# A chunk's output product on TensorE: products of 320 columns in place of pairs of 160

## The chip, the cores and the metric

The kernel runs on one core of a Trainium2 chip. The metric is the device time of one execution in microseconds (us).

## The reference

Two blocks follow each other: a recurrent attention (RWKV-7) and a feed-forward block with the SoLU activation.

```python
# r, k, v, w, a, b: (4, 8, 768, 40) = batch, head, token, channel
for t in range(S):
    y[:, :, t] = einsum('bhd,bhde->bhe', r[t], state)
    Sa = einsum('bhde,bhe->bhd', state, a[t])
    state = state * w[t] - Sa (x) b[t] + v[t] (x) k[t]      # (x): outer product
x = y as (3072, 320)                                        # rows batch*token, columns head*channel
h = x @ w_in                                                # (3072, 1024)
sm = softmax(h)
solu = h * sm
ln = (solu - mean(solu)) / sqrt(var(solu) + 1e-6) * g_ln
out = ln @ w_out                                            # (3072, 320)
```

The change lies in the last product, `ln @ w_out`, of 1024 by 320 for every row.

## The kernel before

**Tiling.** The 768 tokens are cut into chunks of 64 and the four batches into two pairs, so there are 24 steps of work (called `i`), each of which handles 64 tokens of two batches: 128 rows of the output. Inside a chunk the recurrence is solved in closed form with small matrices per head, most of them 64 by 64; TensorE makes them as many small products on quarters of its array (64 rows by 64 columns). The inverse of a triangular matrix that this needs is made on VectorE (`invert`, lines 495 to 526, the groups `prod` and `uu`), a few rows at a time.

**Stages of a chunk.** `norm`, `scores`, `couple`, `close`, `driven`, `solved`, `read` (tiles `py`, `ps`, `px`, `pu`, `pyo`) make the attention. Its result goes through DRAM to be turned (`leave`, `left`). Two steps later `hidden` makes `h`, `highest`, `exped`, `weighed` and `spreadof` make the maximum, the exponentials and the moments, `folded` turns the activations into `lnT` (tiles `plnT`, then `lnT`: eight blocks of 128 by 128), and `output` (lines 845 to 865) makes the output product into the tile `po`. The normalisation's scale is applied when `po` is copied out on ScalarE (line 859, tile `osb`), and two DMAs on the sync queue store the result. g and the mean are folded into the second weight `w2` beforehand: `mean_more` (lines 246 to 255) makes the mean of `w2` with products of 128 by 128 by 320 columns, by the constant matrix `mean`, at about 101 and 121 us.

**The output product.** For each of the eight blocks `f` of 128 hidden columns, `lnT[:, f, :]` (128 by 128) is the stationary matrix and `w2[:, f, :]` (128 by 320) the moving one; the eight accumulate in one PSUM bank. `in_parts` (line 289) cuts such a product into two halves of 160 columns, with the same stationary matrix given twice. The helper `mm` (line 284) issues one product; every product that goes through it carries line 285 in the profile, so that the tiles tell them apart. All data is fp32, and one fp32 product stands in the profile as two weight loads and two matmuls.

**Order of the work.** The order of every engine is written out by hand (`manual_schedule`); nothing is reordered by a planner. In step `i` the chunk whose output is made is `c - 1 = i - 3`. From step 5 to step 22 the eight blocks are cut as six at the end of the step (`FIRST = 6`) and the remaining two in the next step, behind the transposes `pa` and `pkv` (list `rest`); before that and from step 23 on the eight are made at once, in step 25 seven and one. The last chunk is made by `output_last` (line 828), which has halves of its own, in two PSUM tiles, and does not use `in_parts`. `in_parts` is also used in `decay` (line 360, tile `pcum`), for the first steps.

Of the kernel before, what the change touches and what calls it, by code (L numbers as in the profile page):

```python
# [53 lines left out]
def kernel(  # L54
# [25 lines left out]
    NF = DFF // P  # L80
# [60 lines left out]
    w2 = const.tile([P, NF, DM], FP32, name="w2")  # L141
# [126 lines left out]
    def half(p):  # L268
        return slice(C * p, C * p + C)
# [14 lines left out]
    def mm(o, lhsT, rhs, start=True, stop=True):  # L284
        nc.tensor.matmul(o, lhsT=lhsT, rhs=rhs, start=start, stop=stop, skip_group_check=True)  # L285
# [3 lines left out]
    def in_parts(o, lhsT, rhs, start, stop, n=2):  # L289
        width = rhs.shape[-1] // n  # L290
        for x in range(n):
            part = slice(width * x, width * x + width)
            mm(o[:, part], lhsT, rhs[:, part], start and not x, stop)
# [11 lines left out]
    def where_(i):  # L305
        return i % NPAIR, i // NPAIR
# [7 lines left out]
    def ok(i):  # L314
        return 0 <= i < N
# [529 lines left out]
    def output(i, t, first=NF):  # L845
        if not ok(i):
            return
        d = st[i]
        bp, ci = where_(i)
        t = t[:, 0:DM]  # L850

        def products(lo, hi):
            for f in range(lo, hi):
                in_parts(t, d["lnT"][:, f, :], w2[:, f, :], f == 0, f == NF - 1)
        products(0, first)

        def stored():
            osb = two.tile([P, DM], FP32, tag="osb", name="osb", bufs=1)
            nc.scalar.mul(out=osb, in_=t, mul=d["rs"])
            for p in range(2):  # L860
                nc.sync.dma_start(out=out.rearrange("(b s) n -> b s n", b=B)[2 * bp + p, ci * C:ci * C + C], in_=osb[half(p)])
        if first < NF:
            rest.append((lambda: products(first, NF), stored))
        else:
            stored()
# [303 lines left out]
```

## Time and profile before

| what | value |
|---|---|
| time, median of 3 runs | 535.26 us (533.9 to 539.12) |
| span of the profiled execution | 536.5 us |
| instructions | 28053, of them 12029 matmuls and 12029 weight loads |
| TensorE matmul busy | 480.7 us, 90% of the span |
| VectorE, ScalarE, GpSimd busy | 430.6, 314.1, 227.0 us |
| granted TensorE clock, mean | 0.984 |
| matmuls of `po` at line 285 | 768 records of 160 columns, 115.2 us busy |

The profiled execution's span is 1.2 us above the median of the runs and inside their spread. Busy time of an engine is the union of its records; matmuls are pipelined and their ends are modelled, so that records of one run overlap and the pace must be read from the starts. In the lists, `x768` is the number of records, "128\*128 128x160 f32" is the part of the array used and what is streamed or loaded, and a name behind "<-" in the column of idle time is what ended the wait. PE is TensorE's matmuls, PEld its weight loads, DVE VectorE, ACT ScalarE, POOL GpSimd.

### The profile page before, as it was taken

Reading aid. Unit: us, or ns where it says so; the run is one execution under the profiler, and the core shown is the slowest. Engines: PE = TensorE matmul, PEld = TensorE weight load, DVE = VectorE, ACT = ScalarE, POOL = GpSimd, SP = SyncE. Lnnn points to the kernel's source line nnn. Section 1 sums busy time; section 2 is a strip of 40 time slices with the busy share of each in tenths; the row PEclk is TensorE's granted clock in tenths of the full one; section 3 lists DMA queues with packets and bytes.
Section 4 is the critical chain, followed back from the end, with each engine's and each line's share of the span. In section 5 each row is a group of like instructions: output and inputs, shape, how many; then the busy total and the mean of one; then the engine's idle time right before and its main releaser. Section 6 shows DMA issues by size and latency. Waiting matters only on the chain.

```text
span 536.5 us, 28053 instructions
## 1 busy us (share of the span) xinstructions
PE 480.7 (90%) x12029; PEld 391.0 (73%) x12029; DVE 430.6 (80%) x1752; ACT 314.1 (59%) x627; POOL 227.0 (42%) x376
## 2 busy tenths in 40 slices
PE   4633775798989999999999999999999999999997
PEld 3522665665878878877887887788778877887766
DVE  4599987999997987997998979979989888544322
ACT  3633466488457566556666665666656555654433
POOL 4577538245253344545445263544445331210300
PEclk9999978799999999999999999999999999999999
DMA  8898889765465566674774776675554551421210
GB/s 149 153 157 160 177 142 206 165 134 124 90 131 120 102 125 138 123 151 96 147 156 104 132 150 121 118 155 109 114 118 102 108 111 43 106 65 29 61 53 24
DMA packets 194475, 63.95 MB, mean 119 GB/s; under 512 B 166840, under 2 KB 186528, under 8 KB 194352
## 3 DMA queue, kind: packets, MB, share of 16 engines
q1 hardware_dynamic: 181232, 41.60, 41.8%
q0 software_dynamic: 10768, 19.95, 15.2%
q8 instruction: 94, 1.54, 1.2%
q10 hardware_dynamic: 2352, 0.62, 0.7%
q14 instruction: 29, 0.24, 0.2%
HBM read 47.96 MB, written 14.16 MB: 116 GB/s over the span
## 4 chain that ended last, share of the span: by engine, by line
PE 73%; DVE 17%; DMA 5%; issue 2%; ACT 2%; SPq 0%; POOL 0%; ACTq 0%; POOLq 0%; DVEq 0%
PE po L285 20%; PE h L285 18%; PE px L285 6%; PE pyo L285 5%; PE py L285 5%; DVE prod L516 4%; PE ps L285 4%; DVE uu L519 3%; PE pu L285 3%; PE plnT L804 2%; PE pb L400 2%; PE pa L400 2%; PE psr L285 2%; PE pkv L400 2%; DMA uu_dram<-uu 1%
## 5 line engine op out<-in xcount | busy, mean ns | idle before, releaser
L285 PE MATMUL h<-w_in,xT 64*64 64x512 f32 (+1 forms) x1064 | 121.7, 551 | 0.7 <-issue 0.7
L285 PE MATMUL po<-w,lnT 128*128 128x160 f32 x768 | 115.2, 304 | 0.0
L516 DVE TENSOR_TENSOR prod<-blk,uu 128x48 f32<-128x48 f32 (+19 forms) x576 | 108.1, 227 | 1.3
L285 PEld LDWEIGHTS po<-w,lnT 128*128 128x128 f32 x768 | 105.5, 190 | 4.7 <-issue 0.8
L519 DVE TENSOR_TENSOR uu<-uu,prod 128x48 f32<-128x48 f32 (+19 forms) x576 | 103.8, 219 | 0.0
L483 POOL DMA_DIRECT2D nt_dram<-nt x86 | 50.8, 597 | 84.5 <-ACT nt L475 76.4
L792 POOL TENSOR_TENSOR rs<-var,mhalf 128x1 f32<-128x1 f32 x24 | 17.6, 734 | 138.2 <-ACT var L791 138.1
L761 DVE TENSOR_REDUCE nmax<-h 128x1 f32<-128x1024 f32 x24 | 29.3, 1219 | 32.9 <-PE h L285 32.9
L285 PEld LDWEIGHTS h<-w_in,xT 64*64 64x64 f32 x1064 | 36.7, 133 | 20.4 <-issue 16.7
L790 ACT ACTIVATE sq<-e,mu 128x1024 f32<-128x1024 f32 x24 | 26.9, 1119 | 24.4 <-DVE e L777 24.4
L444 DVE TENSOR_TENSOR lu<-pu,cst 128x512 f32<-128x512 f32 x24 | 16.5, 686 | 26.6 <-PE pu L285 24.8
L769 ACT ACTIVATE e<-h,nmax 128x1024 f32<-128x1024 f32 x24 | 26.7, 1111 | 17.7 <-DVE nmax L761 17.7
L558 ACT ACTIVATE wy<-py,cst 128x256 f32<-128x256 f32 x24 | 11.4, 474 | 39.2 <-PE py L285 37.1
L311 POOL DMA_DIRECT2D raw_r<-in_r_dram x48 | 33.3, 698 | 0.0
L777 DVE SCALAR_TENSOR_TENSOR e<-h,e 128x1024 f32<-128x1024 f32 x24 | 29.2, 1217 | 4.3 <-ACT e L769 4.1
L508 DVE SCALAR_TENSOR_TENSOR uu<-blk,uu 128x30 f32<-128x30 f32 (+3 forms) x144 | 30.2, 262 | 1.7 <-DMA blk<-nt_dram 0.8
L393 POOL TENSOR_TENSOR kb<-raw_b,inv 128x320 f32<-128x320 f32 x24 | 21.4, 894 | 21.1 <-DMA raw_b<-in_b_dram 13.7
L285 PE MATMUL pcum<-lw,cst 128*128 128x160 f32 x48 | 15.1, 461 | 16.7 <-ACT lw L351 16.7
L285 PEld LDWEIGHTS py<-tu,nt 64*64 64x64 f32 x768 | 17.3, 142 | 16.3 <-issue 10.7
L617 ACT COPY st<-psr 128x416 f32<-128x416 f32 (+1 forms) x44 | 14.2, 374 | 24.5 <-PE psr L285 24.4
L664 ACT ACTIVATE x<-px 128x832 f32<-128x832 f32 x24 | 20.7, 864 | 11.0 <-PE px L285 11.0
L710 DVE TENSOR_TENSOR tot<-pyo,st 104x416 f32<-104x416 f32 x44 | 23.8, 581 | 2.9 <-PE pyo L285 2.9
(154 smaller groups left out, 1095.3 us busy)
## 6 DMA issues: line engine op xcount, KB each, us to landing
xT<-x_dram SPq DMA_DIRECT2D x48, 160.0 KB, 4.2
blk<-nt_dram POOLq DMA_DIRECT2D x22, 256.0 KB, 4.7
raw_w<-in_w_dram SPq DMA_DIRECT2D x48, 80.0 KB, 3.3
raw_r<-in_r_dram POOLq DMA_DIRECT2D x48, 80.0 KB, 4.0
lv<-in_v_dram SPq DMA_DIRECT2D x48, 80.0 KB, 3.7
out_dram<-osb SPq DMA_DIRECT2D x46, 80.0 KB, 2.5
a<-in_a_dram SPq DMA_DIRECT2D x44, 80.0 KB, 4.0
raw_k<-in_k_dram SPq DMA_DIRECT2D x42, 80.0 KB, 3.8
```

Of the source, the lines that this page charges most:

```text
L285: nc.tensor.matmul(o, lhsT=lhsT, rhs=rhs, start=start, stop=stop, skip_group_check=True)
L311: queue.dma_start(out=x[half(p), :, 0:D], in_=ap[2 * bp + p, :, ci * C:(ci + 1) * C, :].rearrange("h t d -> t h d"))
L400: nc.tensor.transpose(out=t[0:W2, p, at + C * j:at + C * j + C], in_=x[half(p), 2 * j:2 * j + 2].rearrange("p a b -> p (a b)")[:, skip:ski ...
L483: queue.dma_start(out=blocks[n][e].rearrange("(a x h) s c -> a x s h c", a=GRP, x=2)[at, x], in_=nt[home:home + Q].rearrange("p h j c -> p ...
L508: nc.vector.scalar_tensor_tensor(out=u[:, c, j + 1:Q], in0=nb[:, j, j + 1:Q], scalar=u[:, c, j:j + 1], in1=u[:, c, j + 1:Q], op0=ALU.mult, ...
L516: nc.vector.tensor_tensor(out=ts[-1], in0=nb[:, j:j + 1, j + 1:Q].to_broadcast([P, hi - lo, m]), in1=u[:, lo:hi, j:j + 1].to_broadcast([P, ...
L519: nc.vector.tensor_tensor(out=u[:, lo:hi, j + 1:Q], in0=u[:, lo:hi, j + 1:Q], in1=x, op=ALU.add)
L710: nc.vector.tensor_tensor(out=by_b(tot)[:, :, :, part], in0=y[:, :, :, part], in1=by_b(state_of(i)[:, x])[:, :, :, 0:HW], op=ALU.add)
L761: nc.vector.tensor_reduce(out=nmax, in_=d["h"], axis=AX.X, op=ALU.max, negate=True)
L769: nc.scalar.activation(out=e, in_=d["h"], func=AF.Exp, bias=d["nmax"], accum_out=d["esum"])
L777: nc.vector.scalar_tensor_tensor(out=d["e"], in0=d["h"], scalar=1.0 / DFF, in1=d["e"], op0=ALU.mult, op1=ALU.mult, accum_out=d["mu"])
L790: nc.scalar.activation(out=pair("A" if i == N - 2 else "h", "sq").rearrange("p a b -> p (a b)"), in_=d["e"], func=AF.Square, scale=-float( ...
```

## The change

`output` calls `mm` in place of `in_parts`: each of a chunk's eight blocks is one product of 320 columns instead of two of 160. `output_last`, `decay` and the order of the work are as they were.

```diff
         def products(lo, hi):
             for f in range(lo, hi):
-                in_parts(t, d["lnT"][:, f, :], w2[:, f, :], f == 0, f == NF - 1)
+                mm(t, d["lnT"][:, f, :], w2[:, f, :], f == 0, f == NF - 1)
         products(0, first)
```

## The prediction

> **What bounds the kernel now.** I read the page's busy shares and chain first, then TensorE's waits from 180 us on, then the chain of one pair of steps, and last the records of the output product and of the nearest product with 320 columns.
>
> ```profile
> PE 480.7 (90%) x12029; PEld 391.0 (73%) x12029; DVE 430.6 (80%) x1752; ACT 314.1 (59%) x627; POOL 227.0 (42%) x376
> ...
> PE 73%; DVE 17%; DMA 5%; issue 2%; ACT 2%; SPq 0%; POOL 0%; ACTq 0%; POOLq 0%; DVEq 0%
> ...
> L285 PE MATMUL po<-w,lnT 128*128 128x160 f32 x768 | 115.2, 304 | 0.0
> ```
>
> TensorE is on 73% of the chain that ended last, and the output product (po) is the largest single item of its time: 768 records, 115.2 us. Each fp32 product stands in the trace as two loads and two matmuls, so 768 records are 384 products: 23 chunks of 16, and the last chunk's 16, which another function makes and the change leaves alone. The change touches 23 x 32 = 736 records.
>
> Waits of TensorE from 180 us to the end:
>
> ```profile
> PE py L285 <- issue: 0.9, 2, 0.7
> PE ps L285 <- ACT ex L419: 0.3, 1, 0.3
> ```
>
> In 356 us the matmul stream waited 1.2 us in all. Twenty-one of the 23 chunks are made in that stretch, so whatever their products lose or gain there passes to the end nearly one to one. Only the two chunks at 142 and 163 us lie where other engines still hold TensorE up.
>
> The timeline of TensorE around one chunk, and around the only other full-size products of 320 columns (the mean of the second weight, lines 249 and 253):
>
> ```profile
> 312.63 3.53 PE L285 MATMUL po<-w,lnT 128*128 128x160 f32 x24
> 316.09 0.43 PE L400 MATMUL pa<-cst,a 64*104 64x64 f32 x8
> ...
> 317.12 1.35 PE L285 MATMUL po<-w,lnT 128*128 128x160 f32 x8
> ```
> ```profile
> 142.23 4.51 PE L285 MATMUL po<-w,lnT 128*128 128x160 f32 x32
> ```
> ```profile
> 121.23 0.70 PE L253 MATMUL po<-mean,cst 128*128 128x320 f32 x2
> 121.77 1.78 PE L249 MATMUL po<-w,cst 128*128 128x320 f32 x6
> ```
>
> And the durations of single records, from the view of the tile po (minimum, median, maximum in ns):
>
> ```profile
> L285 PEld LDWEIGHTS po<-w,lnT x768: 186/190/190, 142.1 to 532.2; 128*128 128x128 f32 x192
> L285 PE MATMUL po<-w,lnT x768: 299/299/403, 142.2 to 532.3; 128*128 128x160 f32 x192
> ...
> L249 PE MATMUL po<-w,cst x12: 432/432/537, 101.2 to 123.1; 128*128 128x320 f32 x12
> ```
>
> A record of 160 columns lasts 299 ns and one of 320 lasts 432: 160 more columns cost 133 ns, so streaming 160 columns takes 133 ns and the other 166 ns are the pipeline's length, which overlaps from record to record. The pace is what counts. In the unbroken run of 32 it is (4510 - 299) / 31 = 135.8 ns. For 320 columns, from the start of the first at 121.23 to the modelled end at 123.55, it is (2320 - 432) / 7 = 269.7 ns, with a rounding of some 1.5 ns.
>
> **The change part by part.**
>
> *Removed:* 368 matmul records and 368 weight loads (each chunk's 32 pairs become 16), with the same columns streamed. Two records of 160 take 2 x 135.8 = 271.6 ns; one of 320 takes 269.7. That is 2 ns saved a pair. By the other route, a record of 160 takes 135.8 - 133 = 2.7 ns beyond its stream, and one such excess goes away with each pair. Bounds: 0 if the long record carries twice the excess, and 2.7 ns as all that there is beyond the stream. I take 2.5, nearer to the second route, because the first rests on rounded starts: 368 x 2.5 = 0.9 us, with ends of 0 and 1.0 us.
>
> *The weight loads themselves.* A load's row is 190 ns, longer than the pace of 136, so successive loads overlap each other and the matmuls. What a load costs when nothing covers it is read where a chunk begins: 3530 ns for 24 records is 299 + 23 x 135.8 + 108, so the first load of a run lies open for about 105 ns. The maxima agree: 403 against 299, and 537 against 432, are both 104 or 105 more. That opening load stays, once in each run, before and after. The other loads lie beneath the 133 ns stream of the record ahead, at either width. If that cover were gone for the 320-column record alone, the 368 that remain would cost 368 x 104 = 38 us; the run of six at 121.77 speaks against it, though its stationary matrix is the same constant for all six. Against that stand po's own runs, where a new block of lnT is loaded at every fourth record with no break in the pace.
>
> The Trainium skill ("TensorE: Matmul & The Clock Gate", Back-to-back issue gap) would price this otherwise: a stream of load and matmul pairs at 128 columns is given as about 81 ns a pair against 55.6 for the matmul alone, so the load would cost some 25 ns. By that rule the sum would be an estimated 368 x 25 = 9 us of gain instead of 0.9; the pace of 135.8 against a stream of 133 disagrees with it, but its direction is the second rival below.
>
> *The end of a run.* The last record's modelled end lies 432 ns behind its start instead of 299, but that start is one record of 133 ns earlier. Nobody waits longer. The scaling of the output on ScalarE (osb, line 859) waited 3.3 us for po in eight of its 23 times, off the path; it follows the end of the product as before.
>
> *Order, queues, buffers.* No step moves, no DMA is added, the bank and the 320 columns of the accumulator are the same, and the start mark is still set on the first product only. No wait is added. The sequencer of TensorE gets through a chunk with 64 fewer instructions and is further ahead when it leaves it; that can only let the next loads be ready earlier. I cost it at nothing, because po runs at the stream's pace and the waits above show it ready; what it could give at most is the third rival.
>
> *Sum.* The saving of a run of 24 or 8 is the same 2.5 ns per pair. The profiled execution has a span of 536.5 us, 1.2 us above the median of the runs (535.26) and inside their spread (533.9 to 539.12). 536.5 - 0.9 = 535.6 for a like execution; from the median, 535.3 - 0.9 = 534.4 us. That is 0.2%, and the three runs of the unchanged kernel differ by 1% from lowest to highest, so about 1% is what a measurement of this kernel can tell from no change.
>
> **The rivals.**
>
> *First, slower: the clock.* The granted clock fell to half twice:
>
> ```profile
> 66.90:73.70 6.80, 4.42 (x203) 3.90 (x200) 4.65 (x20) 5.90 (x12) 0.00 (x0) 1.00 0.88 162
> 73.70:80.50 6.80, 5.91 (x113) 5.12 (x112) 6.70 (x31) 3.53 (x7) 4.10 (x8) 0.50 0.74 125
> 80.50:90.80 10.30, 5.48 (x216) 4.68 (x216) 10.09 (x25) 9.30 (x21) 8.86 (x14) 1.00 1.01 228
> 90.80:101.00 10.20, 8.81 (x195) 8.16 (x196) 7.45 (x41) 2.91 (x6) 2.54 (x5) 0.50 0.67 131
> 101.00:536.00 435.00, 422.60 (x10779) 341.73 (x10777) 348.77 (x1407) 263.04 (x525) 171.51 (x270) 1.00 0.53 110
> ```
>
> The columns are the window, its length, busy time and records of PE, PEld, DVE, ACT and POOL, then clock, DMA share and GB/s. Each half-clock window follows one with TensorE busy for 65% or 53%. If the grant goes by issued instructions or loads rather than by time spent streaming, then po, at one record every 270 ns, becomes the sparsest stretch of a steady step. It would show first in the tail, where po and h alternate in runs of 4.5 us. A window of 6.8 or 10.2 us at half clock loses 3.4 to 5.1 us; it decides from two windows on, with 8.5 us: 534.4 + 8.5 = 542.9, and three would give 547. For it: nothing in the trace says what the grant counts. Against it: the columns streamed are the same, the eight records of 320 columns at 121 us ran at clock 1.00, and from 101 us on the clock never fell. The same page of the Trainium skill (Part 1, the HAM clock gate) says that the gate follows how busy TensorE was recently, which agrees with the two drops and leaves this rival little.
>
> *Second, clearly faster: loads hold up the array.* If a removed load costs more than its row shows, the gain is 368 times that. One per cent (5.4 us) needs 14.5 ns, 14% of the 104 ns of an open load; a quarter of it, 26 ns, would give 9.6 us and 525.7 us. Against it stands the 2.7 ns beyond the stream, which leaves nothing to take.
>
> *Third, a little faster: issue.* The chain has 3.8% "issue" between 142 and 225 us, 3.2 us, and 0.65 us after that. If all of it were the sequencer being late and 736 fewer instructions ended it, the gain would be 0.9 + 3.8 = 4.7 us: 530.6 us, still inside 1%. The page's queue 8 fetched 94 packets for 1.54 MB; 736 instructions are 3% of TensorE's 24058, so a proportional share is 0.1 us.
>
> *Fourth: cover lost.* The loads of the long records lie open: 535.3 + 38 = 573 us.
>
> **How the numbers follow.** The forecast gets 0.64, the clock 0.18, the second rival 0.07, the third 0.08, the lost cover 0.03. The forecast and most of the third are within 1%; a fifth of the clock's cases have one window only and also fall there; by the runs' spread a tenth of the forecast's own falls outside, half on each side. That makes slower 0.8 x 0.18 + 0.03 + 0.03, some 0.21, rounded up to 0.22, faster 0.07 + 0.03 + a little of the third = 0.11, within 1% 0.67. The unknown price of a pair alone spans 534.3 to 535.3; the runs' spread of 1% around the forecast gives 530 to 540. Up to 543, where the clock's two windows lie, the range holds some 8 in 10.
>
> **What would show it.** In the changed profile: po with 400 records, 368 of 320 columns at 432 ns and the last chunk's 32 of 160 at 299; a run of 12 lasting 3.50 us where 24 lasted 3.53, and 4 lasting 1.34 or 1.35; po's loads down from 768 to 400, now standing apart, so with a busy time near 368 x 190 ns + 4 = 74 us instead of 105.5; PE's waits after 180 us still near 1 us; the clock at 1.00 from 101 us on. Wrong would be: a pace of 320-column records well off 270 ns (second or fourth rival), a window of clock 0.50 after 142 us (first), or TensorE waiting more than 2 us for another engine after 180 us, which no step here provides for.

## Result and profile after: slower by two thirds of a per cent

| kernel | median | lowest to highest | runs |
|---|---|---|---|
| before | 536.36 us | 533.9 to 539.12 | 6 |
| after | 539.92 us | 537.83 to 541.16 | 6 |

The ratio is 1.0065, with a 95% interval of 1.0038 to 1.0092: 3.5 us slower, inside the range of the prediction but on the other side of 1 than the 0.9 us forecast. A second comparison of the same two kernels (after_again, below) gave 1.0093 (1.0066 to 1.012).

What the prediction said of the product itself came out. From the page of after (busy time, the chain, the groups of po):

```profile
PE 481.0 (90%) x11661; PEld 360.5 (67%) x11661; DVE 431.2 (80%) x1752; ACT 314.4 (59%) x627; POOL 225.1 (42%) x376
...
PE 74%; DVE 17%; DMA 3%; ACT 2%; issue 2%; POOL 0%; ACTq 0%; SPq 0%; POOLq 0%; DVEq 0%
...
L285 PE MATMUL po<-w,lnT 128*128 128x320 f32 (+1 forms) x400 | 114.6, 433 | 0.1
...
L285 PEld LDWEIGHTS po<-w,lnT 128*128 128x128 f32 x400 | 71.1, 190 | 27.9 <-issue 1.2
```

There are 368 fewer records of each kind. The loads now stand apart (27.9 us idle before them, 71.1 us busy). The timeline of TensorE around one chunk:

```profile
313.26 3.50 PE L285 MATMUL po<-w,lnT 128*128 128x320 f32 x12
316.69 0.43 PE L400 MATMUL pa<-cst,a 64*104 64x64 f32 x8
...
317.72 1.34 PE L285 MATMUL po<-w,lnT 128*128 128x320 f32 x4
```

3.50 us where 24 records took 3.53, and 1.34 where eight took 1.35. Steps without any pause last 18.42 us after and 18.46 before. So the product gained its 0.04 us a chunk, and the time was lost elsewhere. TensorE's waits from 142 us to the end, first before, then after, show what kind of time; the columns are what waited, what ended the wait, us in total, times, longest:

```profile
PE py L285 <- issue: 2.1, 3, 1.2
PE pst L400 <- DVE bT L440: 0.5, 1, 0.5
PE pst L400 <- DVE aT L427: 0.3, 1, 0.3
PE ps L285 <- ACT ex L419: 0.3, 1, 0.3
```
```profile
PE pyo L285 <- issue: 1.3, 2, 0.8
PE px L285 <- issue: 0.8, 1, 0.8
PE pst L400 <- DVE bT L440: 0.5, 1, 0.5
PE plnT L804 <- ACT sq L790: 0.4, 1, 0.4
PE pst L400 <- DVE aT L427: 0.3, 1, 0.3
PE ps L285 <- ACT ex L419: 0.3, 1, 0.3
PE h L285 <- issue: 0.3, 1, 0.3
PE py L285 <- issue: 0.2, 1, 0.2
```

No wait for another engine has grown much. What stands there is "issue": TensorE stands still and nothing that the profile shows holds it. In this view it grew only from 2.1 to 2.6 us, because it counts a gap from the modelled end of the matmul ahead and leaves out the short ones; read from the starts of the matmuls, the pauses grew more (the table below). They sit in the middle of rows of equal records, first before, then after:

```profile
347.56 0.48 PE L285 MATMUL py<-uh,wy 64*64 64x32 f32 x18
348.69 0.37 PE L285 MATMUL py<-uh,wy 64*64 64x32 f32 x12 [0.65 <-issue]
```
```profile
194.95 0.71 PE L285 MATMUL pyo<-lv,kb 64*64 64x104 f32 x23
196.49 0.48 PE L285 MATMUL pyo<-lv,kb 64*64 64x104 f32 x9 [0.83 <-issue]
```

A row of 32 records of one kind breaks after the 18th or the 23rd, and the profile shows no wait there.

**What the pauses have in common.** Count TensorE's instructions in the trace from the first one on (loads, matmuls, and its sequencer's semaphore instructions): the two pauses above come after number 15552 and number 7105, which are 256 x 60 + 192 and 256 x 27 + 193. The pages of the profile show an instruction queue, q8, with equal packets (queue, packets, MB, share of the engines' time), before and after:

```profile
q8 instruction: 94, 1.54, 1.2%
```
```profile
q8 instruction: 91, 1.49, 1.1%
```

1.54 MB in 94 packets is 16384 bytes a packet. TensorE's stream has 24235 instructions before and 23516 after; 94 x 256 = 24064 and 91 x 256 = 23296, each less than one block short of it. So q8 carries TensorE's instructions, a packet is a block of 256, and the pauses lie at the ends of blocks. From the packets' times in the trace: a packet starts mostly 0.3 to 2.6 us after TensorE passes a boundary, lasts 0.9 to 1.7 us, and TensorE goes on 1.2 to 1.6 us after a packet's end in 87 of the 88 pauses that the twelve traces show between 171 and 482 us (1.9 us in the other). Added up, some 3.8 us pass in the median from a boundary until the next block can be used, a tenth of the times under 3.1 and a tenth over 4.6. A block of 256 instructions that is over sooner than its successor can be used ends in a pause. Of the 790 blocks that end in the 17 steps counted in the table below, 37 of the 73 that lasted under 3.5 us ended in one, 33 of 249 between 3.5 and 4, 18 of 256 between 4 and 5, and none of the 212 longer ones.

Whether it does depends on what lies in the block. Twelve records of 320 columns with their loads are 24 instructions for 3.5 us; 256 successive instructions of small products can be over in 2.7 us. A steady step of before has exactly 1024 instructions, four blocks. They last 5.97, 4.64, 4.12 and 3.73 us, at the same places in every step, and all are longer than 3.6. The change takes 32 instructions out of a step and brings one wait: 993. Now the boundaries move by 31 a step through the work, some blocks last only 3.0 to 3.6 us, and others over 8.

This is theory F. A reckoning with it: the block times of the trace, a delay taken as 3.6 us with a spread of 0.5 us, and the expected excess summed over all blocks from 175 to 495 us. It gives 3.4 us of pauses for before and 8.7 for after: 5.3 more, from which the 0.9 us of the products goes off. Theory P, the rival: the long products hurt in some other way, or the stretches of half clock before 101 us differ. In the two profiles they do, though up to there the programs are the same. The mean clock from 67 to 101 us is 0.75 before and 0.70 after, and 1.00 later (the columns are those of the prediction's windows; first before, then after):

```profile
67.00:101.00 34.00, 24.52 (x725) 21.76 (x722) 28.78 (x113) 21.54 (x44) 15.51 (x25) 0.75 0.83 165
```
```profile
67.00:101.00 34.00, 25.11 (x726) 23.16 (x721) 30.31 (x118) 22.55 (x45) 16.77 (x25) 0.70 0.82 167
101.00:142.00 41.00, 35.50 (x951) 25.29 (x950) 40.55 (x157) 28.39 (x59) 18.64 (x29) 1.00 0.64 137
142.00:225.00 83.00, 79.75 (x2017) 61.05 (x2016) 71.63 (x298) 52.19 (x107) 35.81 (x58) 1.00 0.57 117
225.00:490.00 265.00, 263.85 (x6952) 195.66 (x6954) 221.33 (x931) 161.72 (x321) 108.58 (x173) 1.00 0.54 114
```

Over all runs the clock was no lower in the slower kernels: on average 0.981 in after_again and 0.980 in before on the same chip, 0.983 in before_dec (below) and 0.982 in before beside it. Only before_nosplit lies lower, at 0.978, and its two runs of the lowest clock (0.965 and 0.968) are not its slowest. So the stretches of half clock do not explain the loss.

### The profile page after: what moved, and what is told of

Same layout as the page of the kernel before. It is cut to its first block, busy times and chain, and to the rows that moved or that the text cites. A ratio compares the mean times of both kernels' runs of the same rounds, so it can differ in the third digit from the quotient of the medians.

```text
span 537.4 us, 27334 instructions
## 1 busy us (share of the span) xinstructions
PE 481.0 (90%) x11661; PEld 360.5 (67%) x11661; DVE 431.2 (80%) x1752; ACT 314.4 (59%) x627; POOL 225.1 (42%) x376
## 4 chain that ended last, share of the span: by engine, by line
PE 74%; DVE 17%; DMA 3%; ACT 2%; issue 2%; POOL 0%; ACTq 0%; SPq 0%; POOLq 0%; DVEq 0%
PE po L285 20%; PE h L285 18%; PE px L285 6%; PE pyo L285 6%; PE py L285 6%; PE ps L285 4%; DVE prod L516 4%; DVE uu L519 3%; PE pu L285 3%; PE plnT L804 2%; PE pb L400 2%; PE psr L285 2%; PE pa L400 2%; DVE uu L508 2%; PE pkv L400 2%
## 5 line engine op out<-in xcount | busy, mean ns | idle before, releaser
L285 PE MATMUL h<-w_in,xT 64*64 64x512 f32 (+1 forms) x1064 | 123.4, 552 | 1.3 <-issue 1.3
L285 PE MATMUL po<-w,lnT 128*128 128x320 f32 (+1 forms) x400 | 114.6, 433 | 0.1
L285 PEld LDWEIGHTS po<-w,lnT 128*128 128x128 f32 x400 | 71.1, 190 | 27.9 <-issue 1.2
L792 POOL TENSOR_TENSOR rs<-var,mhalf 128x1 f32<-128x1 f32 x24 | 15.2, 634 | 136.0 <-ACT var L791 136.0
L285 PEld LDWEIGHTS h<-w_in,xT 64*64 64x64 f32 x1064 | 38.8, 134 | 20.7 <-issue 17.4
L285 PE MATMUL ps<-aT,kvT 40*64 40x64 f32 x768 | 17.5, 230 | 11.4 <-ACT kvT L583 11.1
```

## The experiments

In the table, "late part" is read from each trace, from the turning of the first chunk's activations (the first plnT, near 126 us) to the end; "pauses" counts the block boundaries at which the next matmul starts over 130 ns later than the one ahead of it needs for its stream (0.83 ns a column, from the 133 ns for 160), with the sum of these excesses, in the 17 steps of that part that follow the second. Late part and pauses come from one profiled execution each, while the ratio is over all runs.

```
kernel            instructions   ratio to before (95%)       late part   pauses: number, us
                  in a step
before            1024           1                           410.4       2, 1.3
after             993            1.0065 (1.0038 to 1.0092)   411.8       8, 3.4
after_again       993            1.0093 (1.0066 to 1.012)    414.3       10, 4.7
after_lock        1024           1.0031 (1.0009 to 1.0054)   411.6       6, 3.7
after_waits       1025           1.0005 (0.9983 to 1.0026)   409.7       6, 2.1
after_waits_1024  1024           1.0006 (0.9987 to 1.0026)   410.8       8, 3.4
before_s112       1024, moved    1.0327 (1.0302 to 1.0351)   417.2       8, 5.5
before_s256       1024           1.0621 (1.0594 to 1.0649)   411.2       6, 1.9
before_drift      1056           1.0266 (1.0235 to 1.0298)   426.1       18, 11.9
before_dec        1024, moved    1.007  (1.0046 to 1.0093)   411.0       7, 2.1
before_dec_mean   1024           1.001  (0.9993 to 1.0026)   409.8       3, 0.5
before_nosplit    1016           1.0098 (1.0072 to 1.0123)   416.0       6, 4.3
```

### Instructions added by hand (after_lock, before_s112, before_s256, before_drift)

```diff
+    spare = ctx.enter_context(nc.semaphore())
+    def idle(n):
+        for _ in range(n):
+            nc.tensor.sem_inc(spare)
...
# after_lock, in output: after
                 mm(t, d["lnT"][:, f, :], w2[:, f, :], f == 0, f == NF - 1)
+                idle(3 if lo and f == lo else 4)
# before_s112 and before_s256, ahead of the first loads: before
+    idle(112)      # or 256
# before_drift, in output: before
                 in_parts(t, d["lnT"][:, f, :], w2[:, f, :], f == 0, f == NF - 1)
+                idle(4)
```

> The kernel after (320 columns), with the instructions that the change removed from TensorE's stream put back as increments of a semaphore that nobody waits for: four behind each product of 320 columns, three behind the first of each second part, so that each step again has as many TensorE instructions as in the kernel before, 1024, which is four blocks of 256. Theory F (instruction blocks: a step of 1024 keeps the block boundaries at the same favourable places in every step, the step of 992 lets them wander into the densest stretches, where the next block of instructions comes late): the pauses without a wait go back to those of the kernel before and the 0.9 us of the longer products shows: ratio to before 0.998 (0.996 to 1.000). Theory P (the long products themselves cost elsewhere, or the windows of half clock do): it stays at the ratio of the kernel after, 1.0065 (1.004 to 1.009).

> The kernel before with 112 increments of a semaphore that nobody waits for, once, at the very start of TensorE's stream, while it waits for the first loads. The work is that of the kernel before. Theory F: all block boundaries move by 112 instructions to places where, by the trace of before, the four blocks of a step last 3.6, 3.8, 3.0 and 8.0 us instead of 4.1, 3.7, 6.0 and 4.6; with some 3.6 us from one boundary to the next block's arrival that costs 0.7 us a step, so 13 us in 18 steps: ratio 1.024 (1.012 to 1.032). Theory P: nothing changes, ratio 1.000 (0.998 to 1.002).

> The kernel before with 256 such increments at the start, one whole block: all boundaries fall where they fell. Theory F: ratio 1.000 (0.998 to 1.003), the price of the added instructions alone. If the added instructions as such were what slows the kernel with 112 of them, this one would be slowed more than twice as much. Theory P: 1.000.

> The kernel before (pairs of 160) with four such increments behind each pair, so 32 more instructions a step (1056), all beneath the stream of the output product. The products stay as they were; only the boundaries wander by 32 a step, as in the kernel after, the other way. Theory F: the mean over the places costs 0.2 to 0.4 us a step more than the place of before, 4.4 us in all (2.5 to 7): ratio 1.008 (1.004 to 1.013). Theory P: ratio 1.000.

The tool was too coarse. In the traces the increments follow each other at 150 ns, so 112 of them hold TensorE's first product up to 18.0 us and 256 to 40.3 us, where before begins at 6.7. That is most of what both kernels lost: the first plnT comes at 136.0 and 158.7 us instead of 126.2. In the ratios the prediction for before_s256 was missed altogether. The part behind that mark answers the question: 417.2 us with 112 instructions, 411.2 with 256, 410.4 with none (one trace each). The whole block costs 0.8 us, the part of a block 6.8, with eight pauses of up to 1.4 us, all at one place of the step (the instruction numbers are 448 beyond a multiple of 1024), as in this line of the timeline of before_s112:

```profile
364.71 0.40 PE L285 MATMUL pyo<-lu,kb 64*64 64x104 f32 x6 [1.28 <-issue]
```

The 6.8 us are half of the 13 us that I expected. In before_drift the increments take longer (24 x 150 ns = 3.6 us) than the products they were to hide under (3.3 us), so its 15 us are not a clean test; it has the most pauses of all, 18. after_lock went the way of theory F, to half of the loss (the intervals of after_lock and after overlap), but not to 0.998, and its pauses did not go back to those of before: two pauses of 1.0 and 1.9 us near 400 and 415 us make up most of its 3.7 us. Four increments take 600 ns where the product beside them takes 538, so the sequencer loses its lead, and with it the early request for the next block; that reading is argued, not shown.

### Real instructions moved (before_dec, before_dec_mean, before_nosplit)

```diff
# before_dec, in decay
-        in_parts(t, c_("cum"), d["lw"], True, True)
+        in_parts(t, c_("cum"), d["lw"], True, True, n=1 if i < 10 else 2)
# before_dec_mean, besides: in mean_part and mean_more
-            nc.tensor.matmul(t[:, 0:DM], lhsT=c_("mean"), rhs=w2[:, c, :], ...
+            in_parts(t[:, 0:DM], c_("mean"), w2[:, c, :], start and c == lo, stop and c == hi - 1)
-            nc.tensor.matmul(t[:, 0:DM], lhsT=ident, rhs=begun, start=True, stop=False)
+            in_parts(t[:, 0:DM], ident, begun, True, False)
# before_nosplit
-SPLITS = {2: (0, 0, 0, 2, 4), 24: (0, 0, 0, 0, 2)}
+SPLITS = {2: (0, 0, 0, 2, 4), 24: (0, 0, 0, 0, 0)}
```

> The kernel before, with the product of the running sum (decay, tile pcum) of chunks 0 to 9 made as one of 320 columns instead of two of 160: 40 fewer matmul and load instructions and a few fewer waits, all before 165 us, and none after. The output product stays in pairs. Theory F (instruction blocks): less work, but every block boundary of the steady steps falls some 44 instructions further on in the work; from the trace of before, with 3.6 us from a boundary to the next block's arrival, the pauses grow by 6.2 us, and as the same reckoning gave 5.3 us for the kernel after where 4.4 were measured, I expect 5 us: ratio 1.010 (1.005 to 1.015). Theory P (the long output products cost elsewhere): ratio 1.000 or a hair below.

> As before_dec, and the products of the mean of the second weight (lines 249 and 253, at 101 to 170 us) made in pairs of 160 instead of 320 columns: 40 instructions are added again, so that the boundaries of the steady steps fall within four instructions of where they fell in the kernel before. More work than before_dec. Theory F: the pauses go away again, ratio to before 1.000 (0.998 to 1.003), 1% below before_dec. If one product of 320 columns in decay were what slowed before_dec, this one would stay slow.

> The kernel before with the two halved products in the last wave of h (64 rows, 512 columns) made whole again: 8 fewer TensorE instructions a step (1016 instead of 1024). The output product stays in pairs. Theory F: the boundaries wander by 8 a step, 136 in 17 steps, through the same unfavourable places: the reckoning gives 5.1 us more of pauses, by the same correction 4 us: ratio 1.008 (1.003 to 1.013). Theory P: ratio 1.000, or below it by the few ns of each product.

These three leave the output product in its pairs. Taking 40 instructions away, once, in the first third of the kernel, makes it 0.7% slower (1.0046 to 1.0093). Adding 40 elsewhere in that third makes it as fast as it was (0.9993 to 1.0026), though the ten products of 320 columns in decay are still there. Taking 8 away in every step, from a different product, costs 1.0%. All three lie in the ranges expected by theory F, and theory P has no place for any of them: the work that differs is tiny, and only the counts agree. In before_nosplit two boundaries cost 1.2 us each. The trace of before_dec does not show its loss: it has 2.1 us of pauses, 0.8 more than that of before, and comes from the shortest of its twelve runs (537.35 us, the median is 539.98). That its other runs lose their time in pauses is inferred from the ratios.

### The change with its instructions put back cheaply (after_waits, after_waits_1024, after_again)

```diff
     spare = ctx.enter_context(nc.semaphore())
+    nc.tensor.sem_inc(spare)
...
-            nc.tensor.sem_inc(spare)
+            nc.tensor.wait_ge(spare, 1)
...
-                idle(3 if lo and f == lo else 4)
+                idle(7 if lo and f == lo else 8)   # after_waits; two waits make one instruction
+                idle(6 if lo and f == lo else 8)   # after_waits_1024
```

> The kernel after with about 32 instructions a step put back, as in after_lock, but as waits on a semaphore that has long been counted up, in place of increments, which took 150 ns each of the sequencer. Theory F: the steps last 18.42 us with few pauses, and the sequencer keeps its lead, so the late pauses of after_lock go too: ratio to before 0.998 (0.995 to 1.001). Theory P: 1.0065, as the kernel after.

> As after_waits, with one wait fewer in each second part, so that the steps hold 1024 instructions exactly and the boundaries do not wander by the one instruction a step that was left there. Theory F: ratio to before 0.998 (0.996 to 1.000), the 0.9 us of the longer products, and so 0.8% below the kernel after beside it. Theory P: as the kernel after.

> The kernel after, unchanged, once more, beside the next kernel on the same chip, for a second trace of its pauses. Theory F: ratio to before 1.0065 (1.004 to 1.009); pauses at the block boundaries again, in other steps by chance and for other lengths.

With waits that are always met, in 32 instructions a step, the kernel with products of 320 columns is level with before (1.0005 and 1.0006), and 538.32 us against 542.74 for the kernel after beside it on the same chip. Together with the three kernels above, in which the output product stayed as it was, this says that the number of instructions, not the length of the products, made after slower. The 0.2% that I expected below before did not show: both intervals reach to 0.9983 or 0.9987 and leave the question open. So after_waits_1024 came out above its expected range, and after_again (1.0093) just above its own. The pauses did not go away as expected either: the one trace of after_waits_1024 has 8 with 3.4 us, as many as that of after. The lengths of the steps show the gain better: the ten steps from the fifth on last together 3.2 and 5.2 us more than ten steps without a pause in the two traces of after, but 2.4 in after_waits, 2.0 in after_waits_1024 and 0.9 in after_lock; in before it is 2.3. How much a kernel pauses differs from one execution to the next (what makes a block come early or late, the other DMA traffic for one, was not tested), so the conclusion rests on the ratios over all runs. No kernel here is shown to be faster than before: every interval holds 1 or lies above it.

## Why the prediction was wrong

**Right:** the pace of the long records (269 ns, 270 predicted), runs of 3.50 and 1.34 us, 104 ns for each opening load, 400 records and 71.1 us of loads (74 predicted), no new wait for another engine, no half clock after 101 us. TensorE's waits after 180 us, expected near 1 us, were 1.8 us, of which 1.5 "issue" (0.9 before). The saving of 0.04 us a chunk is there in every step without a pause (18.42 against 18.46 us). The first, second and fourth rivals fell with these numbers. None of the signs that the prediction named for being wrong appeared: it looked for a slower pace, a lower clock and waits for other engines, and the loss lay in none of them.

**Wrong step.** It is the paragraph on order, queues and buffers: "The sequencer of TensorE gets through a chunk with 64 fewer instructions and is further ahead when it leaves it; that can only let the next loads be ready earlier. I cost it at nothing". Fewer instructions are not only less work for the sequencer. They change which 256 instructions come in one block, and so whether a block is over before the next has come: where the prediction put nothing, the two traces of after show 2.1 and 3.4 us more of pauses than that of before, and the medians are 3.6 and 4.7 us longer. Even the count was wrong: 16 loads and 16 matmuls are 32 instructions fewer, not 64. The third rival had the place (issue, and queue 8 with its 94 packets) but not the mechanism, and so the wrong sign: it took the share of packets saved, 3%, for the gain. Of the "issue" that it added up, the largest single piece and all of the 0.65 us after 225 us are pauses at block boundaries of before (after instructions 256 x 20 + 192 and 256 x 60 + 192), as the chain of before shows:

```profile
159.54 1.19 issue
```
```profile
348.04 0.65 issue
```

So the mechanism was in the trace before the change, but the view names no cause for it, and it shows only in the instruction numbers. The Trainium skill ("Runtime: NRT & Kernel Launch", Instruction fetch mechanics) has the blocks of 256 instructions, and the packets here agree; it calls the cost of crossing a block's boundary mostly hidden. Here 702 of 790 boundaries show no pause over 130 ns, and the other 88 cost 0.1 to 1.9 us each.

**The size.** The two traces of after have 2.1 and 3.4 us more of pauses than that of before; less the 0.04 us of 17 chunks, 0.7 us, that makes 1.4 and 2.6 us. Their late parts are longer by 1.4 and 3.9 us, the measured medians by 3.6 and 4.7. The first trace fits; in the second 1.3 us, and in the medians more, is not covered by pauses over 130 ns at boundaries. In single steps the excess is 0.1 to 0.2 us more than the pause (at 388 us, 0.87 against 0.65); that the products behind a pause start without their lead would explain it, but is not shown. Whether that is all of the rest stays open.

**The sum's base.** Where both are shown, an execution's time is 2.1 us above its span (539.52 and 537.4). The profiled execution of before, span 536.5, thus stands for some 538.6 us, near the top of that kernel's runs (533.9 to 539.12); the prediction set span and median beside each other and took them for 1.2 us apart. It did not change the sign, but it is one reason why the traces of before and after lie only 0.9 us apart in span where the medians lie 3.6 apart.

## What to carry to other kernels

When TensorE is the bound and makes many small products, its instruction count is part of the layout: find the block boundaries (pauses by "issue" in the middle of a row of equal products, a fixed remainder of the instruction number by 256) and ask how long the shortest block lasts against the delay of a fetch. Removing a few instructions, even once and early in the kernel, can cost more than they did; a loop whose step is a whole number of blocks keeps its boundaries where they are, at good places (before) or bad ones (before_s112), and can be tuned; another wanders through every place. Before blaming an edit, put its instruction count back without its work and see whether the time returns.

## What was new of the hardware

- TensorE's instructions arrive in blocks of 256 (16384 bytes). From passing a boundary to the next block's use took 3.8 us in the median here, of which 0.9 to 1.7 us are the packet and 1.2 to 1.6 us lie behind its end; the shortest blocks were over in 3.0 us, and no block of 5 us or more ended in a pause.
- An increment of a semaphore on TensorE's sequencer takes 150 ns from one to the next (256 in 38.5 us); its record shows 51 ns.
- A fixed offset of some 44 instructions, without any change in the steady steps, moved the time by 0.7%.
